# Regrouping the routing partial sums of batches 1 to 7: turned by VectorE in 32x32 blocks and passed through memory, in the place of transposes on TensorE

## The chip, the cores and the metric

The kernel runs on one core of a Trainium2 chip. Times are device microseconds (us) of that core for one execution. TensorE (PE) multiplies, VectorE (DVE) and ScalarE (ACT) do the elementwise work, GpSimd (POOL) issues the indexed transfers, and SyncE (SP) issues all others. Each engine takes its instructions in the order in which they are written.

## The reference, cut to what matters

```python
x = attention(q, k, v, p)                  # 8 batches of 576 tokens, 512 wide: 4608 tokens
h = x @ w_in; x = (h * sigmoid(h)) @ w_out # dense layer, 512 -> 2048 -> 512
logits = x @ w_gate                        # routing: 8 experts
e_idx = argmax(logits, axis=1)
gate_w = softmax(logits)[e_idx]
eom = 1 / (1 + exp(-(x @ w_output_gate)))
out = gate_w * eom[e_idx] * (relu(x @ w1[e_idx]) @ w2[e_idx])   # token by token
```

The change concerns `x @ w_gate` and `x @ w_output_gate` alone: 16 sums of 512 products for each token.

## The kernel before, in words

**Stages.** `batch(b)` runs eight times, with 16 steps f each. A step multiplies a tile of `w_in` (`mm1`, L796, 12 products into the single buffer `ps_h`), applies the activation (`act`: tanh on ACT at L805, then a product on DVE at L806, which frees `ps_h`), splits the result into two parts (L811 on ACT, L816 on DVE; the leftover tokens at L823 and L825), and multiplies the tile of two steps before by `w_out` (`mm2`, L850, 12 products). So the `mm1` of step f + 1 needs the L806 of step f, and between them PE has the `mm2` of step f - 2. After the batches, `experts` runs the routed experts.

**Work between.** Other work is put into the steps at positions: (f, -2) ahead of `mm1`, (f, -1) behind it, (f, 0) behind the activation, (f, 1) behind `mm2`. `extra_steps` writes that table. In it the attention of batch b + 1 runs as steps s1 to s9 during batch b. For the attention of batches 2 to 7, `s3` (values times weights) stands at (7, 1), `s4` (one transpose of the packed result `pp`) at (8, 0), `s5` (queries times `ppt`) at (9, -2) to (9, 0) and (10, 1), `s6` at (10, 0) and (12, 0). `step_m` (L573, L768, L774), which folds the packed result into the tile of `w_in` for the steps to come, stands at (2, 0), (6, 0) and (10, 0).

**Routing sums.** The tokens of a finished batch (a group of n = 4 blocks of 128, or n = 5 where the leftovers of two batches are added: the groups of odd batches) are stored to memory and read back in 32-row pieces by `regroup`, turned by DVE in 32x32 blocks (`row_x`, L306), and multiplied by the routing weights (`row_products`, L318). The products use four 32-row strips of PE, one for each quarter of the 512 inputs, so there are four partial sums for each token and gate, in strips of partitions: partition 32c + e is gate e of quarter c, and the free axis is the token. `row_part` (L321, ACT) copies this [128, n x 128] from PSUM to `mid`. `row_turns` (L332) turns it on PE, one 128x128 product with the identity for each block, so that tokens are on partitions. `row_add` (L336, DVE) adds the four quarters, and calls `finish` (L868 to L874, then two late parts `pick`, L878 to L880, and `weight`, L885 to L891), which finds the best expert. `place` (15, 0) then sorts the tokens into the experts' lists in memory.

During batches 1 to 6 these parts ride inside the attention steps: `row_products` and `row_part` in `s3`, `row_turns` and `row_add` in `s4`, in spare columns of the same PSUM tile. In batch 7 there is no attention of a next batch, and they are steps of their own: `row_logits` at (7, 1), `row_sum` at (8, 1), `place` at (11, 0). The group of batch 7 itself is treated during the experts, by functions that are not changed.

**SP in batch 7.** There `open_first` prepares the first expert group: behind position (f, 1) of step 4 GpSimd gathers its tokens, and of step 6 `regroup_x` puts 40 small transfers on SP (L275, in `quarters`). Behind step 7 and step 9 it splits weight tiles (`split`, L1102 on ACT, L1103 on DVE), and behind steps 9 and 12 it loads further ones (L1092, L1093 on SP).

Of the kernel before, what the change touches and what calls it, by code (L numbers as in the profile page):

```python
# [8 lines left out]
F32 = mybir.dt.float32  # L9
# [4 lines left out]
ALU = mybir.AluOpType  # L14
AF = mybir.ActivationFunctionType
AX = mybir.AxisListType
# [3 lines left out]
B, H, S, D = 8, 8, 576, 64  # L20
# [10 lines left out]
GB = 5  # L31
# [4 lines left out]
NL = 2 * E8  # L36
# [10 lines left out]
XQ, PART = DM, 6 * DM  # L47
# [41 lines left out]
class Kernel:  # L89
    def __init__(self, tc, ins, out):  # L90
        self.tc, self.nc, self.i, self.out = tc, tc.nc, ins, out
        nc = tc.nc
        self.perm = nc.dram_tensor("perm", (PROWS, PW), I32, kind="Internal").ap()
        self.et = nc.dram_tensor("et", (2, S, 128), F32, kind="Internal").ap()
        self.xr = nc.dram_tensor("xr", (NTOK + 1, DM), F32, kind="Internal").ap()

# [211 lines left out]
    def row_logits(self, g, lo, hi):  # L308
        ps = self.bank("ps_rl")
        self.row_products(g, ps, lo, hi)  # L310
        self.row_part(g, ps, lo, hi)

    def row_products(self, g, ps, lo, hi):
        xt = self.mid[:, :g["n"] * DM].rearrange("p (t c j) -> p c t j", c=4, j=32)
        for i, a in enumerate(range(lo, hi, 4)):
            m = min(hi - a, 4)
            for c in range(4):
                self.nc.tensor.matmul(ps[32 * c:32 * c + 32, i, :m * 128], self.wgt[:, c, :], xt[:, c, 4 * a:4 * a + 4 * m, :], start=True, stop=True)  # L318

    def row_part(self, g, ps, lo, hi):  # L320
        self.nc.scalar.copy(out=self.mid[:, PART + lo * 128:PART + hi * 128], in_=ps.rearrange("p a b -> p (a b)")[:, :(hi - lo) * 128])  # L321

    def row_sum(self, g, lo, hi):
        ps = self.bank("ps_rs")
        self.row_turns(g, ps, lo, hi)
        self.row_add(g, ps, lo, hi)
# [125 lines left out]
    def extra_steps(self, b):  # L452
        sched = {}

        def at(f, pos, fn):
            sched.setdefault((f, pos), []).append(fn)
# [20 lines left out]
        if b > 0:  # L477
            at(1, 1, lambda: self.regroup(self.group))
            for a in range(4 if b % 2 else 5):
                at(*((5, 0), (5, 1), (6, 0), (6, 1), (7, 0))[a], lambda a=a: self.row_x(self.group, a))  # L480
            if b + 1 == B:
                at(7, 1, lambda: self.row_logits(self.group, 0, self.group["n"]))
                at(8, 1, lambda: self.row_sum(self.group, 0, self.group["n"]))
            at(15 if b + 1 < B else 11, 0, lambda: self.place(self.group))
        if b:
            for c in range(1, 4):
# [88 lines left out]
    def att_steps(self, b):  # L575
        nc, pa = self.nc, self.pa
# [79 lines left out]
        def s3(*rs):  # L656
            both = self.psum(b)
            rows = b > 1
            if rows:
                self.row_products(self.group, both, 0, self.group["n"])  # L660
            for r in rs:
                v, ps = self.loads.pop((b, f"v{r}")), both[:, 1, 256 + 64 * r:320 + 64 * r]
                for ch in range(5):
                    for c in range(4):
                        nc.tensor.matmul(ps[32 * c:32 * c + 32, :], a1[r][:, ch, 32 * c:32 * c + 32],
                                         v[:, ch, 64 * c:64 * c + 64], start=(ch == 0), stop=(ch == 4))
            if rows:
                self.row_part(self.group, both, 0, self.group["n"])
            for r in rs:
                nc.vector.tensor_scalar(out=self.pp[:, 64 * r:64 * r + 64], in0=both[:, 1, 256 + 64 * r:320 + 64 * r],  # L670
                                        scalar1=st["sm"][:, 10 + r:11 + r], scalar2=None, op0=ALU.mult)

        def s4():
            both = self.psum(b)
            ps = both[:, 1, 128:256]
            nc.tensor.transpose(ps, self.pp, self.ident)
            if b > 1:
                self.row_turns(self.group, both, 0, self.group["n"])
            ppt = self.p1.tile([128, 128], F32, tag="ppt", bufs=2, name="ppt")
            nc.scalar.copy(out=ppt, in_=ps)  # L680
            self.ppt[b] = ppt
            if b > 1:
                self.row_add(self.group, both, 0, self.group["n"])

        def grp(x):
            return x.rearrange("p a (t n) -> p (a t) n", n=NP)
# [62 lines left out]
        def s9(h):  # L749
            hi, lo = [half(t, h) for t in self.a2[b % 2]]  # L750
            eng = nc.gpsimd if b == 0 or b == 1 and h == 0 else nc.vector
            eng.tensor_tensor(out=lo, in0=st["y"][h], in1=hi.bitcast(F32), op=ALU.subtract)

        steps = {f.__name__: f for f in (s1, s2, s3, s4, s5, s6, s7, s8, s9)}
        return {**steps, "s1": s1_all, "s2": s2_dma, "s5": s5_all} if b > 1 else steps

# [462 lines left out]
```

## Time and profile before

| | |
|---|---|
| median of 3 runs | 1155.51 us (1155.1 to 1161.3) |
| the profiled execution | 1157.25 us |
| its span, first to last instruction | 1154.9 us |
| PE busy | 1129.4 us, 98% of the span |
| DVE, ACT, POOL busy | 654.6, 445.8, 154.4 us |
| mean granted TensorE clock | 0.993 of full speed |
| transfers | 139.64 MB, 121 GB/s on average |

The span is 2.35 us shorter than the execution's own time. A busy PE in this table is counted from the start of a product to its modelled end, so two products that overlap count once. The profile page gives the granted clock in tenths of full speed; in the rows below it is the figure behind the busy times, 1.00 for 2.4 GHz and 0.50 for 1.2 GHz.

### The profile page before, as it was taken

The page shows a single profiled execution, that of the slowest core. Times are in us where ns is not written, and L with a number is a line of the kernel's source. Part 1 is how long each engine was busy: PE and PEld are TensorE (multiplying, and loading weights), DVE is VectorE, ACT ScalarE, POOL GpSimd, SP SyncE. Part 2 cuts the span into 40 slices and gives each one's busy share as a digit, 9 for nine tenths or more (in the row PEclk, how much of TensorE's full clock was granted, in tenths as well). Part 3 has the DMA queues.
Part 4 walks back from the last instruction along what each step waited for, and adds up shares of the span by engine and source line. Part 5 has one row for each costly group of instructions (what it writes and reads, how often), then busy time and mean ns, then how long its engine had stood idle before and what let it go on. Part 6 is the DMA issues. An engine that isn't in the chain of part 4 may idle for free. (4 is left out here: it accounts for less than half of the span.)

```text
span 1154.9 us, 19805 instructions
## 1 busy us (share of the span) xinstructions
PE 1129.4 (98%) x7832; PEld 937.5 (81%) x7832; DVE 654.6 (57%) x1298; ACT 445.8 (39%) x840; POOL 154.4 (13%) x169
## 2 busy tenths in 40 slices
PE   8997999999999999999999999999999999999996
PEld 3556788888888888888888778898999999999995
DVE  5897677357567357567267565374544444454531
ACT  3323534334534334534334443234344343333431
POOL 1202000100100100100100222114130321212021
PEclk9998999999999999999999999999999999999999
DMA  8681346351440441440530342635663645545221
GB/s 325 243 273 54 112 122 95 107 117 42 116 124 8 120 105 42 121 125 1 127 95 1 77 114 88 176 100 164 200 193 103 204 121 176 150 143 155 73 79 43
DMA packets 149510, 139.64 MB, mean 121 GB/s; under 512 B 43041, under 2 KB 123617, under 8 KB 149409
## 3 DMA queue, kind: packets, MB, share of 16 engines
q1 hardware_dynamic: 142112, 118.34, 36.5%
q0 software_dynamic: 7296, 19.96, 5.5%
q8 instruction: 63, 1.03, 0.4%
q14 instruction: 39, 0.31, 0.1%
HBM read 103.97 MB, written 25.11 MB: 112 GB/s over the span
## 5 line engine op out<-in xcount | busy, mean ns | idle before, releaser
L796 PE MATMUL ps_h<-a,mb 128*128 128x288 f32 x1488 | 220.5, 297 | 4.8 <-DVE g L806 4.8
L796 PEld LDWEIGHTS ps_h<-a,mb 128*128 128x128 f32 x1488 | 208.1, 188 | 18.0 <-DVE g L806 5.8
L1133 PE MATMUL pu<-xt,w 128*128 128x256 f32 (+1 forms) x1536 | 215.3, 296 | 0.0
L1133 PEld LDWEIGHTS pu<-xt,w 128*128 128x128 f32 x1536 | 209.5, 190 | 5.1 <-DVE xt L1119 0.2
L850 PE MATMUL acc<-wh,glo 128*128 128x512 f32 x472 | 189.2, 401 | 0.0
L850 PE MATMUL acc<-wh,ghi 128*128 128x512 f32 x472 | 185.6, 393 | 0.0
L850 PE MATMUL acc<-wl,ghi 128*128 128x512 f32 x472 | 185.6, 393 | 0.0
L1158 PE MATMUL py<-w,xt 128*128 128x512 f32 x768 | 185.3, 390 | 0.0
L1158 PEld LDWEIGHTS py<-w,xt 128*128 128x128 f32 x768 | 144.2, 188 | 31.6
L806 DVE SCALAR_TENSOR_TENSOR g<-g,ps_h 128x576 f32<-128x576 f32 x128 | 96.4, 753 | 123.7 <-ACT g L805 122.4
L805 ACT ACTIVATE g<-ps_h 128x576 f32<-128x576 f32 x128 | 83.3, 651 | 182.6 <-PE ps_h L796 160.8
L1139 DVE SCALAR_TENSOR_TENSOR xt<-pu,xt 128x512 fp32r<-128x512 f32 (+1 forms) x128 | 58.7, 459 | 141.8 <-ACT xt L1138 141.8
L1138 ACT ACTIVATE xt<-pu 128x512 fp32r<-128x512 f32 (+1 forms) x128 | 52.5, 410 | 217.7 <-PE pu L1133 167.2
L850 PEld LDWEIGHTS acc<-wh,glo 128*128 128x128 f32 x472 | 89.1, 189 | 39.8 <-issue 16.7
L918 POOL DMA_INDIRECT perm<-pay,dsti x36 | 35.9, 996 | 536.4 <-DVE dsti L916 360.3
L1103 DVE TENSOR_TENSOR w<-raw,w 128x1024 fp32r<-128x1024 f32 x64 | 78.3, 1225 | 46.8 <-ACT w L1102 46.8
L850 PEld LDWEIGHTS acc<-wh,ghi 128*128 128x128 f32 x472 | 89.2, 189 | 19.2
L816 DVE TENSOR_TENSOR glo<-g,ghi 128x512 fp32r<-128x512 f32 x118 | 81.6, 691 | 37.3 <-ACT ghi L811 36.4
L850 PEld LDWEIGHTS acc<-wl,ghi 128*128 128x128 f32 x472 | 89.2, 189 | 15.5
L811 ACT CAST ghi<-g 128x512 fp32r<-128x512 f32 x118 | 73.3, 621 | 65.4 <-DVE g L806 65.2
L1102 ACT CAST w<-raw 128x1024 fp32r<-128x1024 f32 x64 | 66.8, 1045 | 2.3 <-DMA raw<-in_w 2.3
L774 DVE TENSOR_TENSOR mb<-ps_m,mb 128x1024 fp32r<-128x1024 f32 (+1 forms) x34 | 38.4, 1128 | 21.1 <-ACT mb L768 20.9
(230 smaller groups left out, 1047.9 us busy)
## 6 DMA issues: line engine op xcount, KB each, us to landing
raw<-in_w SPq DMA_DIRECT2D x64, 512.0 KB
att_v<-in_v SPq DMA_DIRECT2D x15, 640.0 KB
att_k<-in_k SPq DMA_DIRECT2D x15, 576.0 KB
xr<-xr SPq DMA_DIRECT2D x32, 256.0 KB
mid<-xr SPq DMA_DIRECT2D x32, 256.0 KB
att_q<-in_q SPq DMA_DIRECT2D x14, 576.0 KB
stg<-in_w_out SPq DMA_DIRECT2D x7, 1024.0 KB
xq<-xg SPq DMA_DIRECT2D x112, 64.0 KB
```

The lines of the kernel that those rows point to most:

```text
L796: nc.tensor.matmul(ps[:, hf, :288], lw[:, qd, fs], rx[:, qd, ts], start=(i == 0), stop=(i == 5))
L805: nc.scalar.activation(out=g2, in_=ps[:, :, :288], func=AF.Tanh, scale=0.5)
L806: nc.vector.scalar_tensor_tensor(out=g2, in0=g2, scalar=1.0, in1=ps[:, :, :288], op0=ALU.add, op1=ALU.mult)
L811: self.nc.scalar.copy(out=hi, in_=self.graw[:, :512])
L816: self.nc.vector.tensor_tensor(out=lo, in0=self.graw[:, :512], in1=self.ghi.bitcast(F32), op=ALU.subtract)
L850: self.nc.tensor.matmul(acc, l, r, start=(first and i == 0), stop=(last and i == 2))
L1102: nc.scalar.copy(out=hi, in_=raw)
L1103: nc.vector.tensor_tensor(out=lo, in0=raw, in1=hi.bitcast(F32), op=ALU.subtract)
L1133: nc.tensor.matmul(ps[:, hf, :m], w[:, k, r, fs], xt[:, l, k, ts], start=(i == 0), stop=(i == 11))
L1138: nc.scalar.activation(out=hi, in_=src, func=AF.Relu)
L1139: nc.vector.scalar_tensor_tensor(out=lo, in0=src, scalar=0.0, in1=hi.bitcast(F32), op0=ALU.max, op1=ALU.subtract)
L1158: nc.tensor.matmul(self.acc[j], hl[:, l + j * 128:l + j * 128 + 128], w[:, r], start=(first and i == 0), stop=(last and i == 2))
```

## The change

`row_part`, `row_turns` and `row_add` are no longer used for the groups of batches 0 to 6 (those treated during batches 1 to 7). In their place `row_out` turns the partial sums straight out of PSUM on DVE, in 32x32 blocks: one instruction for 512 columns and, for n = 5, one for the other 128. A block then has tokens on its 32 partitions and the 32 gates of one quarter along the free axis. Four transfers, one for each quarter, write them to a new tensor `lgd` in memory, laid out by token, quarter and gate, in runs of 32 numbers (128 bytes). A fifth reads it back with a token on each partition (runs of 512 bytes). `row_in` adds the quarters out of `mid` and calls `finish`.

In batches 1 to 6, `row_out` stands in `s3` ahead of the two scalings that make `pp`, and `row_in` at (10, 0). In batch 7 `row_whole` (products and `row_out`) stands at (7, 1), and `row_in` at (9, 1). All five transfers are issued by SP.

```diff
+        self.lgd = nc.dram_tensor("lgd", (GB * 128, 4, 32), F32, kind="Internal").ap()
...
+    def row_whole(self, g):
+        ps = self.bank("ps_rl")
+        self.row_products(g, ps, 0, g["n"])
+        self.row_out(g, ps)
...
+    def row_out(self, g, ps):
+        n, ps = g["n"] * 128, ps.rearrange("p a b -> p (a b)")
+        t = self.mid[:, PART:PART + n]
+        for i in range(0, n, 512):
+            self.nc.vector.transpose(out=t[:, i:min(i + 512, n)], in_=ps[:, i:min(i + 512, n)])
+        x = t.rearrange("p (t e) -> p t e", e=32)
+        for c in range(4):
+            self.nc.sync.dma_start(self.lgd[:n, c, :].rearrange("(t j) e -> j t e", j=32), x[32 * c:32 * c + 32])
+        self.nc.sync.dma_start(t.rearrange("p (a x) -> p a x", x=128), self.lgd[:n].rearrange("(a p) c e -> p a (c e)", p=128))
+
+    def row_in(self, g):
+        n = g["n"]
+        self.nc.vector.tensor_reduce(out=g["lg"][:, :n, :], in_=self.mid[:, PART:PART + n * 128].rearrange("p (a c m) -> p a m c", a=n, c=4)[:, :, :NL, :],
+                                     axis=AX.X, op=ALU.add)
+        self.finish(g)
...
             if b + 1 == B:
-                at(7, 1, lambda: self.row_logits(self.group, 0, self.group["n"]))
-                at(8, 1, lambda: self.row_sum(self.group, 0, self.group["n"]))
+                at(7, 1, lambda: self.row_whole(self.group))
+            at(*((9, 1) if b + 1 == B else (10, 0)), lambda: self.row_in(self.group))
...
             if rows:
-                self.row_part(self.group, both, 0, self.group["n"])
+                self.row_out(self.group, both)
...
             nc.tensor.transpose(ps, self.pp, self.ident)
-            if b > 1:
-                self.row_turns(self.group, both, 0, self.group["n"])
...
             self.ppt[b] = ppt
-            if b > 1:
-                self.row_add(self.group, both, 0, self.group["n"])
```

The order of instructions at three places that the prediction speaks of follows. The changed file has lines of its own numbers: up to 22 more than before behind the new functions.

SP in batch 7, before: the 40 transfers of `regroup_x`, then the loads of weights (`raw`).

```order
L1092 DMA raw_6479<-in_w 128x4x256
L1093 ISA
L1093 DMA raw_6480<-in_w 128x2x512
L275 DMA xq_6654<-xs 32x2x128 x32
L275 DMA xq_6654<-mid 32x128 x8
L1092 ISA
L1092 DMA raw_6834<-in_w 128x4x256
```

SP in batch 7, changed.

```order
L1110 DMA raw_6485<-in_w 128x4x256
L1111 ISA
L1111 DMA raw_6486<-in_w 128x2x512
L276 DMA xq_6660<-xs 32x2x128 x32
L276 DMA xq_6660<-mid 32x128 x8
L336 DMA lgd<-mid 32x16x32 x4
L337 DMA mid<-lgd 128x4x128
L1110 ISA
L1110 DMA raw_6837<-in_w 128x4x256
```

The five transfers through `lgd` stand behind all 40 of `regroup_x` and ahead of the next load of weights.

DVE in batch 7, before, from the end of `finish` in step 8 over step 9 into step 10 (`w` is a weight tile, `g` the activation, `mb` is made by `step_m`).

```order
L874 TENSOR_TENSOR oh<-cst,rt 128x32
L806 SCALAR_TENSOR_TENSOR g<-g,ps_h 128x576
L816 TENSOR_TENSOR glo<-g,ghi 128x512
L825 TENSOR_TENSOR gl<-g,gl 128x64
L878 TENSOR_TENSOR mx_6778<-lg,oh 128x32
L879 TENSOR_REDUCE sh<-mx_6778 128x4
L1103 TENSOR_TENSOR w<-raw_6480,w 128x1024
L806 SCALAR_TENSOR_TENSOR g<-g,ps_h 128x576
L774 TENSOR_TENSOR mb<-ps_m,mb 128x1024
```

The same engine and place, changed: step 9, then `row_in` with `finish`, then the split and step 10.

```order
L824 SCALAR_TENSOR_TENSOR g<-g,ps_h 128x576
L834 TENSOR_TENSOR glo<-g,ghi 128x512
L843 TENSOR_TENSOR gl<-g,gl 128x64
L341 TENSOR_REDUCE lg<-mid 128x64
L886 MEMSET oh 128x4
...
L891 TENSOR_TENSOR sh<-mx_6818,lg 128x4x8
L892 TENSOR_TENSOR oh<-cst,rt 128x32
L1121 TENSOR_TENSOR w<-raw_6486,w 128x1024
L824 SCALAR_TENSOR_TENSOR g<-g,ps_h 128x576
L792 TENSOR_TENSOR mb<-ps_m,mb 128x1024
```

The sum that reads `mid` back, and `finish`, now stand between the activation of step 9 and that of step 10.

DVE in step 10 of batch 6 (n = 5), before: `s6`, `step_m`, the split, `s5` and the activation of step 11.

```order
L806 SCALAR_TENSOR_TENSOR g<-g,ps_h 128x576
L723 TENSOR_TENSOR x_5957<-x_5957,mx 128x576
L774 TENSOR_TENSOR mb<-ps_m,mb 128x1024
L816 TENSOR_TENSOR glo<-g,ghi 128x512
L825 TENSOR_TENSOR gl<-g,gl 128x64
L718 TENSOR_REDUCE mx<-x_5957 128x18
L806 SCALAR_TENSOR_TENSOR g<-g,ps_h 128x576
```

The same engine and place, changed.

```order
L824 SCALAR_TENSOR_TENSOR g<-g,ps_h 128x576
L741 TENSOR_TENSOR x_5940<-x_5940,mx 128x576
L341 TENSOR_REDUCE lg<-mid 128x80
...
L892 TENSOR_TENSOR oh<-cst,rt 128x40
L792 TENSOR_TENSOR mb<-ps_m,mb 128x1024
L834 TENSOR_TENSOR glo<-g,ghi 128x512
L843 TENSOR_TENSOR gl<-g,gl 128x64
L896 TENSOR_TENSOR mx_5999<-lg,oh 128x40
L897 TENSOR_REDUCE sh<-mx_5999 128x5
L736 TENSOR_REDUCE mx<-x_5940 128x18
L824 SCALAR_TENSOR_TENSOR g<-g,ps_h 128x576
```

The sum and `finish` moved from step 8 into step 10, between `s6` and `step_m`, and `pick` from the end of step 8 to the end of step 10.

## Rows read from the trace of the kernel before

**Rows 1.** The page, part 1: busy us, share of span and instructions by engine.
```profile
PE 1129.4 (98%) x7832; PEld 937.5 (81%) x7832; DVE 654.6 (57%) x1298; ACT 445.8 (39%) x840; POOL 154.4 (13%) x169
```
**Rows 2.** Groups by line and shape: busy us, mean ns, idle before.
```profile
L332 PE MATMUL ps_s<-cst,mid 128*128 128x128 f32 x27 | 3.9, 272 | 0.0
```
**Rows 3.** Timeline, weight loads (PEld) in s4, batch 6: start, us, instruction, idle before.
```profile
600.83 0.14 PEld L676 LDWEIGHTS ps_s<-cst,pp 128*128 128x128 f32 x1
600.97 0.57 PEld L332 LDWEIGHTS ps_s<-cst,mid 128*128 128x128 f32 x5
601.51 0.19 PEld L850 LDWEIGHTS acc<-wh,glo 128*128 128x128 f32 x1
```
**Rows 4.** Timeline, ACT and DVE in s3, s4 and finish, batch 6 (n = 5).
```profile
599.40 0.69 ACT L321 COPY mid<-ps_s 128x640 f32<-128x640 f32 x1 [2.80 <-PE ps_s L665]
600.13 0.48 DVE L670 TENSOR_SCALAR pp<-ps_s,sm 128x64 f32<-128x64 f32 x2 [2.82 <-ACT mid L321]
...
602.58 0.48 DVE L336 TENSOR_REDUCE lg<-ps_s 128x80 f32<-128x320 f32 x1
...
605.26 0.68 DVE L816 TENSOR_TENSOR glo<-g,ghi 128x512 fp32r<-128x512 f32 x1
...
606.00 0.20 DVE L878 TENSOR_TENSOR mx<-lg,oh 128x40 f32<-128x40 f32 x1
...
606.46 0.24 ACT L880 ACTIVATE sh<-sh 128x45 f32<-128x45 f32 x1 [3.00 <-DVE sh L879]
```
**Rows 5.** Timeline, step 10 of batch 6 into step 12's mm1.
```profile
613.25 0.75 DVE L723 TENSOR_TENSOR x<-x,mx 128x576 f32<-128x576 f32 x1
...
615.65 1.23 DVE L774 TENSOR_TENSOR mb<-ps_m,mb 128x1024 fp32r<-128x1024 f32 x1 [1.65 <-ACT mb L768]
...
617.44 0.65 ACT L805 ACTIVATE g<-ps_h 128x576 f32<-128x576 f32 x1 [1.16 <-PE ps_h L796]
618.19 0.74 DVE L806 SCALAR_TENSOR_TENSOR g<-g,ps_h 128x576 f32<-128x576 f32 x1
...
619.92 1.75 PE L796 MATMUL ps_h<-a,mb 128*128 128x288 f32 x12
```
**Rows 6.** Timeline, SP's queue in batch 7.
```profile
669.96 21.23 SPq L275 DMA_DIRECT2D xq<-xs  x32
691.29 6.04 SPq L275 DMA_DIRECT2D xq<-mid  x8
```
**Rows 7.** Timeline, SP: four writes to memory in runs of 128 bytes, the read behind them.
```profile
579.77 1.98 SPq L652 DMA_DIRECT2D et<-eb  x4
583.28 0.38 SPq L653 DMA_DIRECT2D a1t<-et  x1
```
**Rows 8.** Timeline, DVE and PE in batch 7, finish in step 8 to mm1 of step 11.
```profile
684.07 0.42 DVE L336 TENSOR_REDUCE lg<-ps_rs 128x64 f32<-128x256 f32 x1
...
686.40 0.75 DVE L806 SCALAR_TENSOR_TENSOR g<-g,ps_h 128x576 f32<-128x576 f32 x1
...
688.45 0.22 DVE L825 TENSOR_TENSOR gl<-g,gl 128x64 fp32r<-128x64 f32 x1
...
690.24 1.23 DVE L1103 TENSOR_TENSOR w<-raw,w 128x1024 fp32r<-128x1024 f32 x1 [1.24 <-ACT w L1102]
...
693.74 1.74 PE L796 MATMUL ps_h<-a,mb 128*128 128x288 f32 x12
```
**Rows 9.** Timeline, SP: stores of 256 KB each, and the read that waits for them.
```profile
306.17 1.82 SPq L280 DMA_DIRECT2D xr<-xr  x4
310.57 1.91 SPq L292 DMA_DIRECT2D mid<-xr  x4
```
**Rows 10.** Windows: stretch, length, PE busy, others, granted clock, DMA share, GB/s.
```profile
102.00:103.00 1.00, 1.00 (x8) 1.00 (x7) 1.00 (x2) 0.00 (x0) 0.69 (x1) 0.61 1.07 385
...
106.00:107.00 1.00, 0.32 (x8) 0.26 (x16) 0.97 (x3) 0.00 (x0) 0.00 (x0) 0.50 0.00 0
...
112.00:113.00 1.00, 1.00 (x5) 0.81 (x5) 0.84 (x2) 0.00 (x0) 0.29 (x1) 0.77 0.00 0
```

## The prediction, made before the changed kernel was run

> **What bounds the kernel now.** I read the page's busy times first [rows 1]: PE is busy for 98% of the span, the next engine for 57%. So whatever leaves PE is a gain if nothing else makes it wait, and whatever makes PE wait is a loss in full. Then I looked for where PE comes near to waiting. A step of a batch is `mm1` and `mm2`. The `mm1` of a step needs the DVE product L806 of the step before, which frees `ps_h`. In [rows 5] L806 of step 11 ends at 618.19 + 0.74 = 618.93 and the `mm1` that needs it starts at 619.92: 0.99 us to spare. A delay of DVE by more than that is a delay of the kernel. Last I read SP's queue in batch 7 [rows 6] and the place where the sums are used there [rows 8], since the change sends data through that queue.
>
> **The change, part by part.** The sums below are made on the profiled execution (1157.25 us, span 1154.9) and are added at the end to the median, 1155.51, as differences.
>
> *Products removed.* The turns of the 7 groups are 27 products in `s4` [rows 2] and 4 in batch 7. Their mean duration is 272 ns, but they overlap: the five weight loads start at 600.97 and the next product's load at 601.51 [rows 3], so one costs 0.54 / 5 = 0.108 us of PE. Batches 1 to 6: 27 x 0.108 = **2.9 us less**. The 4 of batch 7 (0.4) fall into the wait below and give nothing. The Trainium skill ("TensorE: Matmul & The Clock Gate", Part 4: PE-mode transpose) gives about 275 ns for a 128x128 transpose in a kernel. By it the 27 would be worth 7.4 us, and the sum would come out 4.5 lower. The spacing of the rows decides, and I take 0.108.
>
> *From s3 to s4.* Before, ACT copies (0.69) and then DVE makes `pp` (0.48), ready at 600.61 [rows 4], and PE wants it at 600.83 [rows 3]. Now DVE turns 640 columns itself. No row here has a block turn out of PSUM; from DVE's 0.75 for 576 columns [rows 5] I estimate some 0.65 for 512 and 0.25 for 128 more. 599.40 + 0.90 + 0.48 = 600.78. That fits by a hair; for n = 4 it fits with 0.3 to spare. I take 0, at most 0.2 for each n = 5. ACT loses a copy, which nobody waits for elsewhere.
>
> *The trip through memory, batches 1 to 6.* Four writes of 128-byte runs take SP 1.98, and the read behind them is issued 583.28 - (579.77 + 1.98) = 1.53 later [rows 7]; its issue takes 0.38, and landing between 1.5, as these writes, and 2.6, as 306.17 + 1.82 to 310.57 shows for larger stores [rows 9]. From 600.3 that gives 606 to 607. `row_in` comes up on DVE behind L723, at 614.0 [rows 5]. 7 us to spare: hidden. On SP the read's wait holds up only loads for the next batches, which have tens of us.
>
> *Sum and finish moved from step 8 to step 10.* They take 605.26 - 602.58 = 2.68 for n = 5 [rows 4], and 686.40 - 684.07 = 2.33 for n = 4 [rows 8]. In step 10 DVE is idle for 1.65 ahead of L774, waiting for ACT [rows 5]; that hides part. The rest, 1.03 or 0.68, delays L774 and all behind it. Then comes `pick`: two instructions of 0.20, 0.46 from the first to the exponential on ACT that waits for them, 0.24 [rows 4]. ACT's queue has the tanh of step 11 behind it. So for n = 5: L723 ends 614.0, finish 616.7, L774 and the two splits 618.6, `pick` 619.05, exponential 619.3, tanh 0.65 to 619.95, L806 to 620.7. That is 1.8 later than 618.93, against 0.99 to spare: PE waits 0.85. For n = 4 the same chain is 0.35 shorter: 0.5. Three groups of each: 2.55 + 1.5 = **4.0 us more**. The later steps (`weight`, 0.9, now in step 11) just fit by the same working. Bounds: 0 if ACT gets ahead, 5 if steps 12 and 13 wait too. The old place in step 8 gives nothing back: there they stood behind L806, and no wait of PE in the trace follows from them.
>
> *Batch 7.* Here is the large term. SP issues 40 transfers from 669.96 to 691.29 + 6.04 = 697.33 [rows 6], 0.66 us each for 32, then some more; in program order `row_out`'s five stand behind them, though its turns on DVE come two steps ahead of 688.6, and a step is 691.38 - 686.40 = 5.0 [rows 8] or less: done by about 680. Their trip then is: four writes at 0.57, as writes here also wait for older ones, to 699.6; landing 1.5 to 701.2; read 0.38; landing 2.3, near the larger stores of [rows 9], as 256 KB are read: 703.9. DVE comes to `row_in` after L825 of step 9, 688.6 [rows 8], and stands for some 15 us. Behind it on DVE: finish 2.33 to 706.25, L1103 about 1.15 to 707.4, L806 of step 10, 0.75, to 708.15. PE meanwhile runs `mm1` and `step_m` of step 10 and the `mm2` behind, until just before 693.74, and then waits for that L806. Its `mm1` started at 693.74 [rows 8] and would start at 708.2: **14.5 us more** (13.0 with landings of 1.5 and issues of 0.5; 16.5 with landings of 2.6 and waits for older writes). SP's start there rests on earlier work of the same core, so it shifts with PE and the sum stands.
>
> *Clock.* PE will idle for nearly 15 us, and no row here has so long a lull. After a shorter lull around 100 us the granted clock fell to 0.5 at about 102.6; PE took up work again at 106.7, and the clock was full again at about 112.5 [rows 10]. 5.8 us of work at 1.2 GHz in the place of 2.4 cost **2.9 us more**. Bounds: 0 if it does not fall, 5 if the lull meets it worse.
>
> Sum: -2.9 + 4.0 + 14.5 + 2.9 = +18.5. Span 1154.9 to 1173.4, execution 1157.25 to 1175.75, median 1155.5 to **1174.0 us**.
>
> **The rivals.** *The queue does not hold the trip up* (not slower). If issuing cost SP little, the five transfers would leave at 680 and be back at 686, ahead of 688.6; batch 7 would cost nothing, and the clock neither. Time: 1155.5 - 2.9 + 4.0 - 0.4 = 1156.2, within the bound. It decides itself at the point where SP is through with the 40 before about 681. The Trainium skill ("DMA: Bandwidth & Descriptors", Issuing engines are not separate DMA queues) says that the time a sequencer takes to start a transfer is usually small beside the transfer, and by that rule this would be the outcome. The trace disagrees: 40 issues take 27.4 us [rows 6]. *The same, without waits in step 10*: 1155.5 - 3.3 = 1152.2, still within the bound; only a dearer price of the removed products would make it faster than that. *Only the long wait*: DVE and ACT make room in step 10 and the clock stays up, 1155.5 - 2.9 + 14.5 = 1167.1. The 0.99 to spare speaks against the first, [rows 10] against the second. *Everything at its upper bound*: 1155.5 - 2.9 + 5 + 16.5 + 5 = 1179.1.
>
> **How the numbers follow.** What a measurement of this kernel can tell from no change is about 0.5%, 5.8 us: 1149.7 to 1161.3. The forecast and its near neighbours have 0.70 (1170 to 1177), only the long wait 0.13, the upper bounds 0.08, the queue that does not hold 0.05, and without waits in step 10 0.03; 0.01 is left for faster still. So faster 0.01, same 0.08, slower 0.91. The range reaches from the lower bounds taken together, 1155.5 - 2.9 + 13.0 = 1165.6, to the upper ones: 1166 to 1179.
>
> **What would show it.** In the changed profile the chief sign is the sum L341 on DVE in batch 7: idle for about 15 us ahead of it, put down to the transfer into `mid`, and PE idle just as long ahead of step 11's `mm1`, with a granted clock of 0.5 after it. SP must show the four `lgd` writes right behind the last of the 40. In batches 1 to 6, step 12's `mm1` should follow 0.5 to 0.85 of idle PE, released by DVE, and L774's wait for ACT should be gone; PE should have 31 products fewer in 128x128. I am wrong if SP gets through the 40 earlier, if DVE is free before 688.6 + 5, or if PE finds work in the wait.

## The result and the profile after

The changed kernel takes 1173.89 us (median of 5 runs, 1172.21 to 1175.17), the kernel before 1155.79 in the same series: ratio 1.014, 95% interval 1.0112 to 1.0168. It is slower by 18 us, close to the 1174.0 foretold. The sum behind that number is not as good as the number, and that the two meet within 0.1 us is in part luck: two of its terms missed in opposite directions, and two experiments below show that the clock's part was misunderstood.

The page, busy us and share of the span by engine (after; answers to [rows 1]), whose head gives a span of 1172.1 us:

```profile
PE 1127.5 (96%) x7798; PEld 934.1 (80%) x7801; DVE 659.6 (56%) x1308; ACT 440.3 (38%) x833; POOL 150.9 (13%) x169
```

PE is busy for 1.9 us less in a span that is 17.2 us longer. The work went down; the time went into waits. Most of it is one wait. SP's queue in batch 7 (timeline of after, start, us; answers to [rows 6]):

```profile
670.09 21.68 SPq L276 DMA_DIRECT2D xq<-xs  x32
691.87 4.99 SPq L276 DMA_DIRECT2D xq<-mid  x8
697.29 1.97 SPq L336 DMA_DIRECT2D lgd<-mid  x4
700.92 0.38 SPq L337 DMA_DIRECT2D mid<-lgd  x1
```

The four writes of the partial sums (L336) start at 697.29, right behind the last of the 40 transfers of `regroup_x`, and the read (L337) follows 1.66 after their end. What that does to DVE and PE (timeline of after, the same stretch as [rows 8], which showed the `mm1` of step 11 at 693.74):

```profile
688.38 0.22 DVE L843 TENSOR_TENSOR gl<-g,gl 128x64 fp32r<-128x64 f32 x1
...
703.91 0.59 DVE L341 TENSOR_REDUCE lg<-mid 128x64 f32<-128x256 f32 x1 [15.32 <-DMA mid<-lgd]
...
706.35 1.22 DVE L1121 TENSOR_TENSOR w<-raw,w 128x1024 fp32r<-128x1024 f32 x1
707.49 0.75 DVE L824 SCALAR_TENSOR_TENSOR g<-g,ps_h 128x576 f32<-128x576 f32 x1
...
708.29 3.25 PE L814 MATMUL ps_h<-a,mb 128*128 128x288 f32 x12 [14.46 <-DVE g L824]
...
714.39 1.75 PE L814 MATMUL ps_h<-a,mb 128*128 128x288 f32 x12
```

DVE is free at 688.6 and stands for 15.32 us in front of the sum, whose data come by DMA. The split L1121 and the activation L824 of step 10 are queued behind it, and PE waits 14.46 us for that activation. Its twelve products then take 3.25 us, in the next step 1.75. The granted clock says why (windows of after: stretch, length, busy us of PE, PEld, DVE, ACT, POOL, granted clock, DMA share, GB/s; the counterpart of [rows 10]):

```profile
700.00:702.00 2.00, 0.00 (x0) 0.00 (x0) 0.00 (x0) 0.00 (x0) 0.00 (x0) 0.50 0.15 24
...
710.00:711.00 1.00, 1.00 (x6) 1.00 (x5) 0.39 (x3) 0.23 (x1) 0.00 (x0) 0.50 0.52 201
711.00:712.00 1.00, 1.00 (x10) 0.81 (x9) 0.00 (x0) 0.36 (x1) 0.00 (x0) 0.73 0.07 16
712.00:713.00 1.00, 1.00 (x6) 0.80 (x5) 0.68 (x2) 0.29 (x1) 0.00 (x0) 1.00 0.34 50
```

The clock is still full over the first 4 us of the wait (0.97 over 696 to 698, 0.50 from 698 on); it is at half (1.2 GHz) over the rest of it and over the first 3.2 us of work behind it (708.29 to about 711.5).

The other loss is small and comes six times. Timeline of after, step 10 of batch 6 into step 12 (answers to [rows 5]):

```profile
613.57 0.74 DVE L341 TENSOR_REDUCE lg<-mid 128x80 f32<-128x320 f32 x1
...
616.51 1.22 DVE L792 TENSOR_TENSOR mb<-ps_m,mb 128x1024 fp32r<-128x1024 f32 x1
...
618.60 0.20 DVE L897 TENSOR_REDUCE sh<-mx 128x5 f32<-128x40 f32 x1
618.72 0.74 DVE L736 TENSOR_REDUCE mx<-x 128x18 f32<-128x576 f32 x1
...
618.84 0.24 ACT L898 ACTIVATE sh<-sh 128x45 f32<-128x45 f32 x1 [2.91 <-DVE sh L897]
618.98 0.63 ACT L823 ACTIVATE g<-ps_h 128x576 f32<-128x576 f32 x1
...
619.65 0.76 DVE L824 SCALAR_TENSOR_TENSOR g<-g,ps_h 128x576 f32<-128x576 f32 x1 [0.19 <-ACT g L823]
...
620.46 1.86 PE L814 MATMUL ps_h<-a,mb 128*128 128x288 f32 x12 [0.72 <-DVE g L824]
```

The sum waits for nothing (its data are there), but `finish` behind it ends at 616.5. The split L792 starts 0.86 later than before (1.2 counted from `s4`, where this run is 0.35 ahead), without the 1.65 of idle ahead of it. `pick` comes later by as much, and ACT, which takes its instructions in order, holds the tanh (L823) until the small exponential of `pick` (L898) has its operand: 618.98 where it was 617.44. DVE itself is busy until L736 ends at 619.46 and then waits 0.19 for that tanh. PE waits 0.72; the ledger below has 0.88, since it counts from where the product would have started, ahead of the modelled end of the one before it.

**The ledger.** I compared the start of each step's first product between the two traces and noted every change of the difference (us, added up from the first changed place in batch 1 to the experts):

| place | before to after |
|---|---|
| `s4` of batches 1 to 6: -0.43 for each n = 4, -0.55 for each n = 5 | -2.94 |
| steps 12 and 13: +0.51 for each n = 4, +0.99 for each n = 5 | +4.50 |
| batch 5, a wait of PE for a load of v that is only in the profile before | -0.65 |
| batch 7, step 1, a wait for DVE of 1.90 before and 1.64 in after | -0.25 |
| batch 7, step 8: four products fewer | -0.44 |
| batch 7, step 11: the long wait | +14.62 |
| batch 7, step 12: the clock | +1.52 |
| experts, a wait for data read from memory (L307) | +0.77 |
| sum | +17.13 |

The span grew by 17.2. The third and the eighth row are not the change's: two kernels below whose batch 5 is as before (seven_alone, products_twice) don't have the wait of 0.65 either, and PE's wait of the eighth row is 0.25 before and 1.03 in after, but 0.39 and 0.43 in wait_filled and wait_filled_early, which have the same change, and 1.31 in forty_behind_trip, which is 17 us faster than after. The fourth row goes with the change: one instruction of DVE in that stretch (L207 in before, part of the choice of the first expert) takes 0.47 us in before, seven_alone and products_twice and 0.21 where batches 1 to 6 are changed; why stays open. The profiled runs are up to 2.9 us apart by the time batch 1 begins (products_twice and before), ahead of anything that the change touches, so single medians can't settle tenths; the ledger, which takes the differences step by step, can.

### The profile page after: what moved, and what is told of

It reads as the page before. It is cut to its first block, busy times and chain, and to the rows that moved or that the text cites. A ratio compares the mean times of both kernels' runs of the same rounds, so it can differ in the third digit from the quotient of the medians.

```text
span 1172.1 us, 19782 instructions
## 1 busy us (share of the span) xinstructions
PE 1127.5 (96%) x7798; PEld 934.1 (80%) x7801; DVE 659.6 (56%) x1308; ACT 440.3 (38%) x833; POOL 150.9 (13%) x169
## 3 DMA queue, kind: packets, MB, share of 16 engines
q8 instruction: 63, 1.03, 0.4%
## 5 line engine op out<-in xcount | busy, mean ns | idle before, releaser
L824 DVE SCALAR_TENSOR_TENSOR g<-g,ps_h 128x576 f32<-128x576 f32 x128 | 96.1, 751 | 124.9 <-ACT g L823 124.9
L823 ACT ACTIVATE g<-ps_h 128x576 f32<-128x576 f32 x128 | 83.2, 650 | 201.7 <-PE ps_h L814 164.2
L1121 DVE TENSOR_TENSOR w<-raw,w 128x1024 fp32r<-128x1024 f32 x64 | 78.3, 1224 | 42.9 <-ACT w L1120 29.6
L792 DVE TENSOR_TENSOR mb<-ps_m,mb 128x1024 fp32r<-128x1024 f32 (+1 forms) x34 | 38.3, 1126 | 10.5 <-ACT mb L786 10.3
```

Of the source, the lines that this page charges most:

```text
L823: nc.scalar.activation(out=g2, in_=ps[:, :, :288], func=AF.Tanh, scale=0.5)
L824: nc.vector.scalar_tensor_tensor(out=g2, in0=g2, scalar=1.0, in1=ps[:, :, :288], op0=ALU.add, op1=ALU.mult)
L1121: nc.vector.tensor_tensor(out=lo, in0=raw, in1=hi.bitcast(F32), op=ALU.subtract)
```

## The experiments

My theory: the order in SP's queue makes the long wait, the half clock follows from PE's idleness, and ACT's order makes the six small waits. Rivals: the trip itself is slow or the memory is loaded; the loss comes from batches 1 to 6; DVE's own time makes the small waits.

**1. Where the time is: batch 7 undone, and batch 7 alone.** In seven_undone batch 7 uses the old functions.

```diff
-                at(7, 1, lambda: self.row_whole(self.group))
-            at(*((9, 1) if b + 1 == B else (10, 0)), lambda: self.row_in(self.group))
+                at(7, 1, lambda: self.row_logits(self.group, 0, self.group["n"]))
+                at(8, 1, lambda: self.row_sum(self.group, 0, self.group["n"]))
+            else:
+                at(*(10, 0), lambda: self.row_in(self.group))
```

> The changed kernel with batch 7 as before (copy by ScalarE, four products, sum at (7, 1) and (8, 1)); batches 1 to 6 keep the trip through memory. Theory (the trip of batch 7 is queued on SP behind 40 transfers and costs the wait and the slow clock behind it; batches 1 to 6 come out nearly even, 2.9 us of products saved against some 4.5 us of waits in step 12): 1156 us, 1155 to 1158, with the six waits of TensorE ahead of step 12 still there, 0.2 or 0.7 us each. Rival (turning and passing through memory costs in every batch, by VectorE's time or by its 128-byte runs): most of the 18 us stays, 1162 or more.

Measured 1155.70 us beside 1156.88 (ratio 0.9988, 0.9973 to 1.0003). In seven_alone it is the other way round: batches 1 to 6 use `row_part`, `row_turns` and `row_add`, and only batch 7 is changed.

```diff
-            at(*((9, 1) if b + 1 == B else (10, 0)), lambda: self.row_in(self.group))
+                at(9, 1, lambda: self.row_in(self.group))
...
-                self.row_out(self.group, both)
+                self.row_part(self.group, both, 0, self.group["n"])
...
+                self.row_turns(self.group, both, 0, self.group["n"])
...
+                self.row_add(self.group, both, 0, self.group["n"])
```

> The kernel before with the change in batch 7 alone. Theory: the whole loss is here, 14.6 us of wait, 1.5 of slow clock, some 0.8 at the first products of the experts, less 0.4 for four products: 1172.3 us, 1170.5 to 1174, and VectorE idle for about 15 us ahead of the sum. Rival (the loss is spread over the batches): clearly under 1170.

Measured 1172.85 (1.0135, 1.0104 to 1.0166), with 14.75 in the ledger at step 11 and 2.15 for the clock. The large loss is batch 7's. Batches 1 to 6 are about even by the medians, and 1.6 us to the bad by the ledger (-2.94 + 4.50): seven_undone has the six small waits and the saved products as in the ledger, seven_alone has neither.

**2. Is it the order of the queue?** In seven_on_gpsimd GpSimd issues the five transfers of batch 7.

```diff
+        q = self.nc.gpsimd if g["b"] == B - 2 else self.nc.sync
...
-            self.nc.sync.dma_start(self.lgd[:n, c, :]...
+            q.dma_start(self.lgd[:n, c, :]...
-        self.nc.sync.dma_start(t.rearrange(...
+        q.dma_start(t.rearrange(...
```

> The changed kernel with the five transfers of batch 7 issued by GpSimd, which is idle there, and not by SP. Theory (the place in SP's queue is the cause): the first write is issued at about 680, not 697; GpSimd took 1.0 us for an indexed transfer of 128 rows, so the four writes and the read are through by 690 to 695, and VectorE waits 1 to 6 us and not 15: 1158 to 1166 us. Rival (short runs are slow to land, whoever issues them): from the last write's issue to the read's landing much more than the 5 us seen on SP, and VectorE's wait stays near 15.

A single execution took 1154.61 us. Timelines of seven_on_gpsimd, first GpSimd, then DVE:

```profile
679.26 2.69 POOL L337 DMA_DIRECT2D lgd<-mid  x4 [8.05 <-DVE mid L333]
684.87 0.78 POOL L338 DMA_DIRECT2D mid<-lgd  x1 [2.92 <-DMA xq<-xs]
...
688.26 0.61 DVE L342 TENSOR_REDUCE lg<-mid 128x64 f32<-128x256 f32 x1 [0.91 <-DMA mid<-lgd]
```

The same trip, while SP is at its 40 transfers, takes 9.0 us from the first write to the sum, and DVE waits 0.91 instead of 15.32. I had expected more to be left of the wait. The same kernel again, over 12 executions:

> The kernel of seven_on_gpsimd again, timed in rounds: its one look gave 1154.6 us, 1 us below the kernel before. The gains of the products left out (some 3.4 us over batches 1 to 7) and the waits of step 12 (4.5 us) leave it within 2 us of the kernel before: 1154 to 1157 us.

1154.81 beside 1155.98 (0.999, 0.998 to 1.000): as expected, and as fast as before. forty_behind_trip leaves everything on SP and exchanges the order only:

```diff
         elif f == 6:
...
-            self.regroup_x(0)
         elif f == 7:
             self.split(0, 1)
+            self.regroup_x(0)
```

> The changed kernel with one thing moved: in batch 7 the 40 transfers that regroup x are issued behind the trip of the partial sums instead of ahead of it, on the same queue. If the 15 us are a matter of order in SyncE's queue (theory), the sum finds its data within about 3 us, and the 40 transfers now end some 8 us later, about 711 us; the turns of x in steps 13 to 15 may wait 1 to 2 us for them: about 1157 us (1155 to 1159). If instead the trip itself is slow, or the memory is loaded (rival), the sum still waits 10 us or more: about 1170 us.

Timelines of forty_behind_trip, SP and then DVE:

```profile
679.39 1.97 SPq L336 DMA_DIRECT2D lgd<-mid  x4
683.00 0.38 SPq L337 DMA_DIRECT2D mid<-lgd  x1
683.49 21.48 SPq L276 DMA_DIRECT2D xq<-xs  x32
705.08 5.28 SPq L276 DMA_DIRECT2D xq<-mid  x8
...
687.66 0.62 DVE L341 TENSOR_REDUCE lg<-mid 128x64 f32<-128x256 f32 x1
```

Now the sum waits for nothing, and the 40 transfers end at 710.4, 13.5 us later than in after; in the ledger no product up to the experts starts later for that. Measured 1156.86 (1.0006, 0.9995 to 1.0017). The 14.62 and the 1.52 are both gone, by order alone. The rival (a slow trip, loaded memory) is out as the cause of the 15 us: from the first write to the sum it is 6.6 us in after, 9.0 beside the 40 on another queue, and at most 8.3 here.

**3. The consumer moved instead.** In seven_late the trip stays behind the 40, and `row_in` of batch 7 goes to (13, 1), `place` to (15, 0).

```diff
-            at(*((9, 1) if b + 1 == B else (10, 0)), lambda: self.row_in(self.group))
-            at(15 if b + 1 < B else 11, 0, lambda: self.place(self.group))
+            at(*((13, 1) if b + 1 == B else (10, 0)), lambda: self.row_in(self.group))
+            at(15 if b + 1 < B else 15, 0, lambda: self.place(self.group))
```

> The changed kernel with the sum of batch 7 at (13, 1) and the placing at (15, 0), in the place of (9, 1) and (11, 0); the transfers stay where they are, behind the 40. Theory (what costs is who waits, not the trip): the trip is back at about 704 while step 13 ends later than that, so the wait goes, but VectorE has a turn of the expert group in step 13 too and may be late by up to 1 us: 1156.5 us, 1155.5 to 1158. Rival (the transfers themselves disturb the others, for instance the 40, whose data step 13 needs): 3 us or more stay, 1159 and up.

Measured 1158.02 (1.0015, 0.9998 to 1.0032): the long wait is gone, and another has come. Timeline of seven_late, PE:

```profile
711.74 1.86 PE L814 MATMUL ps_h<-a,mb 128*128 128x288 f32 x12 [1.90 <-DVE g L824]
```

Sum, finish and two turns of x for the expert keep DVE from 705.73 to 709.70. ACT's cast of the turned x waits for those turns, and the tanh stands behind the cast, so DVE waits another 1.23 for the tanh and comes to the activation at 710.93. PE waits 1.9 there (2.06 in the ledger), and 0.7 comes on top a step later. I had allowed 1. The rival has no part in it: the 40 take SP 26.5 us here (668.84 to 695.37) and 26.8 in after.

**4. Is the term of the removed products right?** products_twice is the kernel before with each turn of batches 1 to 7 made twice.

```diff
+            for _ in range(2 if g["b"] < B - 1 else 1):
                 self.nc.tensor.transpose(ps[:, i * 128:i * 128 + 128], self.mid[:, at:at + 128], self.ident)
```

> The kernel before with each of the 31 turning products of batches 1 to 7 made twice. Theory (one costs the 0.108 us by which they follow one another): 3.3 us more, 1159.1 us, 1158.5 to 1160. Rival (one costs its mean duration of 0.27 us): 8.4 us more, 1164.

Measured 1159.97 beside 1156.14 (1.0031, 1.0019 to 1.0043): 3.8 us for 31 products, or 0.12 each; in the ledger about +0.40 for each 4 and +0.55 for each 5, 0.10 to 0.11 each. The spacing of weight loads is the price. By their duration of 272 ns ([rows 2]) the 31 would have cost 8.4, and the interval ends at 5.0.

**5. The small waits.** sum_in_step_9 puts the sum of batches 1 to 6 one step earlier, at (9, 1), with batch 7 as before.

```diff
             else:
-                at(*(10, 0), lambda: self.row_in(self.group))
+                at(*(9, 1), lambda: self.row_in(self.group))
```

(shown against seven_undone)

> Batches 1 to 6 with the trip through memory and the sum at (9, 1) in the place of (10, 0); batch 7 as before. Theory (the waits in step 12 come from the sum and finish being put into the fullest stretch of VectorE): at (9, 1) VectorE is idle for 1.5 us and the step behind has a folding product that gives 1 us more room, the trip has been back for 4 us, so the waits go and the 2.9 us of products stay as gain: 1152.9 us, 1152 to 1154. Rival (the waits come from ScalarE's queue, tanh behind the exponential of pick, which stays in step 10): half of the waits stay, 1154.5 to 1156.

That was wrong: 1156.87 beside 1156.14 (1.001, 1.0001 to 1.0019), and the waits in the ledger are what they were or a little more, 0.42 and 0.91 (0.39 and 0.88 in after). Timelines of sum_in_step_9, DVE and then ACT (this kernel's own lines: L826 is the activation, L794 the split of `step_m`, L900 the exponential of `pick`, L825 the tanh):

```profile
612.52 0.75 DVE L826 SCALAR_TENSOR_TENSOR g<-g,ps_h 128x576 f32<-128x576 f32 x1
613.19 0.75 DVE L743 TENSOR_TENSOR x<-x,mx 128x576 f32<-128x576 f32 x1
615.59 1.23 DVE L794 TENSOR_TENSOR mb<-ps_m,mb 128x1024 fp32r<-128x1024 f32 x1 [1.65 <-ACT mb L788]
...
613.98 0.69 ACT L744 ACTIVATE x<-x 128x576 f32<-128x576 f32 x1 [2.72 <-DVE x L743]
...
617.93 0.24 ACT L900 ACTIVATE sh<-sh 128x45 f32<-128x45 f32 x1 [1.70 <-DVE sh L899]
618.07 0.63 ACT L825 ACTIVATE g<-ps_h 128x576 f32<-128x576 f32 x1
```

`finish` now delays the activation of step 10 (612.52), which delays the next product on DVE, and with it ACT's exponential and cast, on which L794 waits its 1.65 as before. Moved by a step, the work only entered the same chain further ahead: the idle time of DVE ahead of the split hangs on DVE's own product, and can't be filled from in front. `pick` still stands ahead of the tanh. step_9_and_late joins this with seven_late:

```diff
-            at(*((9, 1) if b + 1 == B else (10, 0)), lambda: self.row_in(self.group))
+            at(*((13, 1) if b + 1 == B else (9, 1)), lambda: self.row_in(self.group))
-            at(15 if b + 1 < B else 11, 0, lambda: self.place(self.group))
+            at(15 if b + 1 < B else 15, 0, lambda: self.place(self.group))
```

> The trip through memory in all seven batches, the sum at (9, 1) in batches 1 to 6 and at (13, 1) in batch 7 with the placing at (15, 0). Theory: 31 products less and no wait but up to 1 us in step 13 of batch 7: 1152.5 us, 1151.8 to 1154. Rival as in the run with batch 7 late: 3 us more, by transfers in one another's way.

1157.65 (1.002, 1.0011 to 1.0028), a miss by the same two errors. pick_after_13 takes `pick` away from in front of the tanh. It is seven_on_gpsimd with `pick` put off by three steps in batches 1 to 6.

```diff
-        self.late.append(pick)
+        def later(n, fn):
+            self.late.append((lambda: later(n - 1, fn)) if n else fn)
+
+        later(3 if g["b"] < B - 2 else 0, pick)
```

> seven_on_gpsimd with one more thing moved: in batches 1 to 6 the pick (and the weighting behind it) runs three steps later, behind step 13, so that its exponential no longer stands on ScalarE ahead of step 12's tanh. If ScalarE's order is what makes step 12's first product wait (theory), the six waits of 0.5 and 0.99 us go to 0.1 or less and 3 to 4 us are gained on gpsimd_timed: about 1152.5 us. If VectorE's own time ahead of the eviction is what makes it late (rival), the waits stay at 0.4 to 0.9 us and the time with them: about 1156 us.

Timeline of pick_after_13, step 10 of batch 6 to step 12, and the `mm1` of step 1 of batch 7 (L824 is the tanh, L825 the activation, L815 `mm1`):

```profile
613.72 1.22 DVE L793 TENSOR_TENSOR mb<-ps_m,mb 128x1024 fp32r<-128x1024 f32 x1
...
614.30 0.65 ACT L824 ACTIVATE g<-ps_h 128x576 f32<-128x576 f32 x1 [1.16 <-PE ps_h L815]
...
615.58 0.75 DVE L737 TENSOR_REDUCE mx<-x 128x18 f32<-128x576 f32 x1
...
616.25 0.74 DVE L825 SCALAR_TENSOR_TENSOR g<-g,ps_h 128x576 f32<-128x576 f32 x1
...
617.05 1.85 PE L815 MATMUL ps_h<-a,mb 128*128 128x288 f32 x12
...
642.63 2.42 PE L815 MATMUL ps_h<-a,mb 128*128 128x288 f32 x12 [2.21 <-DVE g L825]
```

The tanh waits 1.16 for PE, as in [rows 5], and for nothing else, and is done before DVE comes to the activation. In the ledger the waits of step 12 fall from 0.39 to 0.00 (n = 4) and from 0.88 to 0.26 (n = 5). But the run takes `pick` off two engines, its exponential off ACT and its two instructions off DVE, and the timelines tell the two apart. From the start of the split of `step_m` to the activation DVE takes 3.14 in after (616.51 to 619.65) and 2.53 here (613.72 to 616.25), 0.61 less. Of that, 0.26 lies behind the start of L736 (here L737): 0.93 from there to the activation in after, 0.67 here. That is ACT's order. The other 0.35 lies ahead of it and is `pick`'s own time on DVE. The last 0.26 that PE still waits is `finish` on DVE, for the activation now follows L737 without a gap. So where n = 5 ACT's order is 0.26 of the 0.88, and the rival, DVE's own time, has the larger part. Where n = 4 (batch 5) the two parts are 0.26 and 0.33 against a wait of 0.39, so that by these figures each alone would have removed most of it. A kernel in which ACT's order alone is changed was not run.

But the time is 1154.97 (0.9987, 0.9977 to 0.9998), no better than gpsimd_timed. Of some 3.3 us gained in steps 12 and 13, 1.0 is lost again at step 0 of the five next batches (0.15 to 0.27 each), and the rest at the start of batch 7. There DVE chooses the first expert ahead of an activation, and PE waits for it at step 1, 1.90 before and 1.64 in after, at full clock on both sides. In pick_after_13 DVE comes 0.57 later, the wait is 2.21, and the windows show what follows (columns as above):

```profile
641.00:642.00 1.00, 0.00 (x0) 0.00 (x0) 0.86 (x7) 0.00 (x0) 0.31 (x1) 1.00 0.05 15
...
643.00:644.00 1.00, 1.00 (x9) 1.00 (x8) 0.74 (x2) 0.37 (x2) 0.86 (x1) 0.83 0.00 0
644.00:645.00 1.00, 1.00 (x6) 1.00 (x5) 0.09 (x1) 0.00 (x0) 0.10 (x1) 0.50 0.04 8
...
647.00:648.00 1.00, 1.00 (x6) 0.83 (x5) 0.74 (x2) 1.00 (x4) 0.12 (x1) 0.96 0.04 8
```

The clock is at half over 3.4 us of work, and the next `mm1` is another 1.55 late (1.0 + 0.57 + 1.55 = 3.1 given back). The theory was right that the waits would go with `pick`; that ACT's order was the reason holds for a part of them only, and on the gain it was wrong. Putting `pick` off in batches 1 to 5 only was not tried.

**6. The clock behind the long wait.** Both kernels are the changed one with 104 products whose result is never read, so that PE has work in the wait. In wait_filled they stand at (10, 1).

```diff
+    def fill(self):
+        ps, x = self.bank("ps_w"), self.tri.rearrange("p a b -> p (a b)")
+        for _ in range(104):
+            self.nc.tensor.matmul(ps[:, 0, :256], x[:, :128], x, start=True, stop=True)
...
+            if b + 1 == B:
+                at(10, 1, self.fill)
```

> The changed kernel with 104 products of 256 columns on a constant, which nobody reads, put ahead of the wait of TensorE in batch 7. Theory (14.5 us of idle time let the clock fall, and 3.2 us of work behind it ran at 1.2 GHz): the products take about 11 us of the wait, the granted clock stays at 1.00 there, and 1.5 us come back: 1172.4 us, 1171.5 to 1173.5, with the wait's end where it was. Rival (the clock falls for another reason, or the work behind the wait is slow for another): no gain, 1173.9.

1184.87 (1.0255, 1.0237 to 1.0274). Timeline of wait_filled, PE:

```profile
707.34 13.07 PE L187 MATMUL ps_w<-tri 128*128 128x256 bf16 x104 [15.37 <-DVE mb L799]
```

My placement was wrong: the bank still held what the split of `step_m` on DVE had to read, and that stands behind the sum. The products ran after the wait, not in it, and the median is 11 us above that of after. In wait_filled_early they stand at (10, 0), ahead of `step_m`.

```diff
-                at(10, 1, self.fill)
+                at(10, 0, self.fill)
```

(shown against wait_filled)

> The changed kernel with 104 idle products (their result is not read) that TensorE makes ahead of step 10's own work in batch 7, into a bank that is free, so that TensorE is busy over most of the 15 us wait. They change nothing that is computed. If the half clock behind the wait comes from TensorE's idleness (theory), the granted clock stays at 1.00 over 700 to 713 us and the 1.5 us behind the wait come back, while the wait's end stays: about 1172.4 us (1171.5 to 1173.5). If the clock behind the wait costs nothing that counts, or the idle products delay step 10's own (rival), 1173.9 us or more.

The median is 1172.31 (1.0147, 1.0131 to 1.0163), as the theory said, but what the theory said of the clock did not come. Timeline of wait_filled_early, PE (L820 is `mm1`):

```profile
687.90 11.53 PE L187 MATMUL ps_w<-tri 128*128 128x256 bf16 x104
...
706.72 3.25 PE L820 MATMUL ps_h<-a,mb 128*128 128x288 f32 x12 [3.20 <-DVE g L830]
```

and its windows (columns as above):

```profile
705.00:706.00 1.00, 0.00 (x0) 0.00 (x0) 1.00 (x2) 0.00 (x0) 0.00 (x0) 1.00 0.00 0
706.00:707.00 1.00, 0.28 (x1) 0.28 (x2) 1.00 (x3) 0.30 (x1) 0.00 (x0) 0.87 0.00 0
...
709.00:710.00 1.00, 1.00 (x11) 0.85 (x9) 0.00 (x0) 0.12 (x1) 0.00 (x0) 0.50 0.01 2
710.00:711.00 1.00, 1.00 (x9) 0.87 (x7) 0.25 (x1) 0.65 (x1) 0.00 (x0) 0.93 0.00 0
```

PE was idle for 3.20 us instead of 14.46. The clock stayed full through that wait, but fell all the same, just as the work began again, and the twelve products took the same 3.25 us. The ledger has +14.86 and +1.58, against 14.62 and 1.52 in after: nothing was saved. The profiled run (1171.67) is shorter than after's because it reached batch 1 already 1.8 us earlier (-2.03 against -0.22 in the ledger), ahead of anything that differs; that the median's 1.6 comes from the same is likely and not shown. Three us of idleness cost what fourteen do, and the 2.21 of pick_after_13 cost as much; behind waits of 1.64 (after), 1.90 (before, batch 7) and 1.90 (seven_late) the clock stayed at 1.00. That waits of PE bring the half clock is borne out by forty_behind_trip, where the long wait is gone and the half clock with it. Whether the idle products, in bf16, count as others do stays open, and with it what would have happened had they filled the last 3.2 us too.

## Why the prediction was right, step by step

- **Products removed, -2.9.** Right: -2.94 in the ledger, and products_twice shows 0.10 to 0.11 each. [rows 3] carried it, not the duration of [rows 2]. The page has 31 weight loads fewer, as foretold; of products it has 34 fewer, since three records (L182, a loop of start-up products) are missing from the trace of after.
- **From s3 to s4, 0.** Right, and the estimate for the block turns, 0.65 + 0.25, came out at 0.91. Timelines of after, batch 6, first DVE, then weight loads:

```profile
599.60 0.91 DVE L333 STREAM_TRANSPOSE mid<-ps_s 128x512 f32<-128x512 f32 x2 [2.09 <-PE ps_s L687]
600.44 0.43 DVE L692 TENSOR_SCALAR pp<-ps_s,sm 128x64 f32<-128x64 f32 x2
...
601.03 0.14 PEld L698 LDWEIGHTS ps_s<-cst,pp 128*128 128x128 f32 x1
601.16 0.19 PEld L868 LDWEIGHTS acc<-wh,glo 128*128 128x128 f32 x1
```

  `pp` is ready at 600.87, PE takes it at 601.03; where five loads stood there is now nothing. The estimate could have been a reading: the trace of before has block turns out of PSUM (L708, two of 512 columns in 1.31 at 606.44), though none of the rows shows one.
- **The trip of batches 1 to 6, hidden.** Right: L341 has no wait there.
- **Steps 10 to 12, +4.0.** The mechanism was right in each link (`finish`, split, `pick`, exponential, tanh, activation); the size was 4.5. Step 12 waits 0.88 and 0.39 where 0.85 and 0.5 were forecast (by the forecast's own times, 620.7 - 618.93 - 0.99, it is 0.78, and 0.43 for n = 4); the rest is 0.11 in step 13, six times, where I had said that it "just" fits. I ended the chain with ACT; for n = 5, 0.26 of the 0.88 remains when `pick` is gone from both engines, as DVE is late by itself.
- **Batch 7, +14.5.** Right: 14.62, and the sum at 703.9 to the tenth. The parts were less exact: the writes began at 697.29 (697.33 foretold) and took 1.97, not 2.28; the read was issued 1.66 behind them (1.5); it landed in 2.6, not 2.3. They cancel.
- **Four products of batch 7, 0.** They are gone in step 8 (-0.44), but the wait ends by SP's queue, which doesn't follow PE's gain within two steps (its 40 transfers begin at 670.09, ahead of step 8, and run on to 697.29); the ledger's 14.62 is counted from the earlier start. As forecast, they give nothing.
- **Clock, +2.9.** Too much: 1.52. I took the 5.8 us that [rows 10] need to full clock; here it took 3.2 behind PE's first product, 4.6 in seven_alone (2.15 lost). And its reason, "nearly 15 us" of idleness, is not needed: 2.2 and 3.2 us did as much. The trace of before had it already. In [rows 10] PE is busy for 1.00 of the stretch 102 to 103, and the mean clock of 0.61 puts the fall at about 102.2 (not 102.6): while PE worked, a microsecond behind a wait of 2.90. Timeline of before, PE:

```profile
101.20 2.43 PE L796 MATMUL ps_h<-a,mb 128*128 128x288 f32 x12 [2.90 <-DVE g L806]
```

- **Sum.** +18.5 foretold; in the ledger the change's own rows are -2.94 + 4.50 - 0.25 - 0.44 + 14.62 + 1.52 = +17.0, 1.5 less. The clock alone is 1.4 less; the small waits and the long one are 0.6 more, and the two small rows of batch 7 are 0.7 less, of which the 0.25 of step 1 was not foreseen. So the mechanism held, and the size was 1.5 us off. That the medians differ by 18.1, and so by almost the forecast, is luck in part: the runs of after alone spread over 3 us.
- **The rivals.** "The queue does not hold the trip up" was put at 1156.2; seven_on_gpsimd and forty_behind_trip, which make it true, give 1154.8 and 1156.9. Beside that rival stood a sentence of the Trainium skill ("DMA: Bandwidth & Descriptors", Issuing engines are not separate DMA queues), that the time a sequencer takes to start a transfer is usually small beside the transfer. What counted here was not one start beside one transfer, but forty starts in a row: 40 small transfers occupied SP for 27.2 us ([rows 6], and 670.09 to 697.29 here), about 0.64 each, and five others behind them paid 15. How long a single one of the 40 took to land no row shows, so for one transfer the sentence is not tested here.

## What to carry to other kernels

What a transfer cost here was its place in a queue, not its size: before routing data through memory, look up what its issuing engine has in front of it there, in that stage. The same five transfers cost 15 us behind 40 others, nothing ahead of them, and some 0.3 us of PE on another engine's queue. Work that is moved on a busy engine is to be followed through every later instruction that hangs on it, for a step earlier can be the same chain. And where a median agrees with a forecast, the trace must still show the forecast's reason: here one forecast had the number without the reason (wait_filled_early), and one found the waits but not the gain (pick_after_13).

## What was not expected of the hardware

- Waits of TensorE of 2.21 and 3.20 us were followed by the half clock over 3.4 us of work each, as one of 14.46 was over 3.2, at the same price of 1.5 to 1.6 us. With the short ones the clock fell only when the work had begun again (0.83 over 643 to 644, 0.87 over 706 to 707), as in [rows 10] behind a wait of 2.90 (0.61 over 102 to 103). Waits of 1.64 and 1.90 were followed by full clock.
- From the first product to the full clock it took 3.2 (after), 3.4 (wait_filled_early) and 4.6 us (seven_alone) with the same work at that place, and 5.8 in [rows 10].
- The block turns out of PSUM cost DVE 0.91 for 640 columns (512 and 128); those that before had already (L708, 512 columns) take 0.70 each in the mean. The sum of the quarters out of SBUF costs 0.74 (n = 5) and 0.59 to 0.62 (n = 4), where out of PSUM, in another layout, it cost 0.48 and 0.42 ([rows 4, 8]).
- GpSimd issues these plain transfers in 0.67 us each (2.69 for four), against 0.49 on SP (1.97; in seven_late the same four took SP 3.05). GpSimd's times are the rougher ones in these profiles.
